# The second mixture's first 128 rows computed with w1 as the moving operand, and a split of the scatters ahead of them

## The chip, the cores and the metric

The kernel runs on one core of one Trainium2 chip. The metric is the device time of one execution in microseconds (us), the median of several executions. Before the change it is 572.95 us, the median of 3 runs (572.11 to 574.3).

## What is computed

Three stages follow each other: a decayed linear attention, a mixture of experts with one expert for each token, and a second such mixture in which tokens with a positive skip score are computed and the others pass through.

```python
def _attn_ref(q, k, v, alpha):            # B, H, S, D = 4, 8, 768, 48
    for t in range(S):
        state = alpha[:, :, t, :, None] * state + einsum('bhd,bhe->bhde', k[:, :, t], v[:, :, t])
        y[:, :, t] = einsum('bhd,bhde->bhe', q[:, :, t], state)

def _moe_ref(x, w_gate, w_output_gate, w1, w2):   # 3072 tokens, D 384, 8 experts, F 1024
    e_idx = argmax(x @ w_gate, axis=1)
    for e in range(E):
        mask = e_idx == e
        ye = np.maximum(x[mask] @ w1[e], 0.0) @ w2[e]
        out[mask] = gate_w[mask, None] * eom[mask, e, None] * ye

def _moe2_ref(x, w_skip, w_gate, w1, w2):
    out = x.copy(); xc = x[x @ w_skip > 0]        # only these are computed
    # the same routing; y[mask] = gate_w * (relu(xc[mask] @ w1[e]) @ w2[e]); out = xc + y
```

## The kernel before

The attention takes the first 150 us or so, in chunks of 128 positions. While it ends, tokens are routed, and each token's row (384 values, its weight and its index) is scattered by GpSimd's indirect DMA to its expert's region of a buffer in HBM: `scr1` for the first mixture, `scr2` for the second. Both mixtures then work through one list, `ITEMS`. An item is a number of rows of one expert: load them (`load_rows`, a DMA of SyncE's queue, L368), transpose and split them in a high and a low part (`xsplit`, or `xsplit_small` for items with one row block, L404 on TensorE, L405 and L406 on ScalarE and VectorE), multiply by w1 and take the relu (layer 1), multiply by w2 (layer 2), and then the steps that follow. Every product is three: high by high, low by high, high by low.

Counted from zero, the items that matter here are these. Item 8 is expert 7 of the first mixture, the last one there, with 432 rows in 4 row blocks of 108. Item 9 is expert 0 of the second mixture, its first 128 rows. Item 10 is the next 128 rows of the same expert. Item 11 is expert 1 of the second mixture with 256 rows. Item 9's rows are loaded while item 8 is being computed, and none of them comes from item 8; rows of item 10 are among those that item 8's results are scattered to.

So there is a chain from item 8 to item 10, and it runs through item 9. `post1_steps` makes the steps that follow an item of the first mixture, in groups, and `stream` runs them inside the next item: group 0 ahead of layer 1, and each further group behind a piece of it. For item 8 (`quick`) the groups are: copy the result (`evac`); logits, row block 0 (`rows(0)`, L517 and L521), routing and weights; row blocks 1 and 2 and the places (`place`: the rank by small matmuls, L190 to L196, then the indices `pi`, L560, and `ski`); row block 3 and the scatters (L224), four to `scr2` and four to the output. Item 10's load stands on SyncE's queue behind the fourth scatter to `scr2`, and TensorE's transposes for item 10 (L404) stand behind item 9's layer 2.

Layer 1 has two forms. In the usual one (`layer1`, L431) a block of w1 is the stationary operand and the rows move: 8 blocks of F, each 9 matmuls of as many columns as there are rows, here 128. In the form by rows (`layer1_rows`, L449) the 128 rows are stationary and w1 moves: 2 halves of F, each 9 matmuls of 512 columns. Its result lies with rows on the partitions, so it is copied (`hr`, L695) and each half is turned by 4 transposes (`layer1_turn`, L456, then `hh` L461 and `hl` L462). Before the change item 10 runs by rows, item 9 does not. Layer 2 (L487) is the same for both, 24 matmuls of 384 columns.

In a by-rows item the loop of `stream` runs group 1 behind the first half, group 2 behind the second, and group 3 inside layer 2, behind its first piece (f = 0); the usual form runs group g behind block g - 1 of F. The order on each engine is that in which the code is written; engines wait for each other by semaphores alone.

Of the kernel before, what the change touches and what calls it, by code (L numbers as in the profile page):

```python
# [51 lines left out]
def kernel(  # L52
# [170 lines left out]
    def scatter(dst, idx, j, src, pp, bound, key=None):  # L223
        ins = nc.gpsimd.indirect_dma_start(  # L224
            out=dst, out_offset=bass.IndirectOffsetOnAxis(ap=idx.bitcast(U32)[0:pp, j:j + 1], axis=0),
            in_=src, in_offset=None, bounds_check=bound, oob_is_err=False,
        )
        if key is not None:
            if groups[key]:
                tc.declare_no_dep(ins.ins, group=key, reason="the rows differ")  # L230
            tc.add_to_no_dep_group(key, ins.ins)
            groups[key].append(ins)
# [9 lines left out]
    def turn_logits(sm_ps, lt, gg, pp):  # L242
        nc.tensor.transpose(sm_ps[0:pp, 128:128 + gg * LW], lt[0:gg * LW, 0:pp], ident[0:gg * LW, 0:gg * LW])
# [121 lines left out]
    def load_into(xr, it, g0=0, g1=None):  # L365
        first, e, base, pp, gg = it
        r0, g1 = e * CAP + base, g1 or gg
        nc.sync.dma_start(  # L368
            out=xr[0:pp, 0:g1 - g0],
            in_=(scr1 if first else scr2)[r0:r0 + pp * gg, :].rearrange("(p g) d -> p g d", p=pp)[:, g0:g1],  # L370
        )

    def load_rows(it):
        xr = mp.tile([128, G1, PAY], F32, name="xr", bufs=2)
        load_into(xr, it)
        return xr
# [63 lines left out]
        )  # L440

    def in_rows(it):
        return it[4] == 1 and it[2] > 0

    def layer1_rows(ws, xhl, c, ph, k0, k1):
        terms = [(kb, w, x) for kb in range(KB) for w, x in ((ws[0], xhl[0]), (ws[1], xhl[0]), (ws[0], xhl[1]))]
# [45 lines left out]
    def post1_evac(py, it, quick):  # L492
        n = it[3] * it[4]
        yt = mp.tile([128, KB, N1], F32, name="yt")
        for d in range(KB):
            if quick and d == 1:
                nc.vector.tensor_copy(yt[:, d, 0:n], py[d])
            else:
                nc.scalar.activation(out=yt[:, d, 0:n], in_=py[d], func=AF.Copy)
        return yt  # L500

    def post1_logits(yt, it):
        pp, gg = it[3:]
        smp = psM.tile([128, 512], F32, name="smp")
        for d in range(KB):
            for g in range(gg):
                nc.tensor.matmul(  # L507
                    smp[g * LW:(g + 1) * LW, 0:pp], wg2s[:, d], yt[:, d, g * pp:(g + 1) * pp],
                    start=(d == 0), stop=(d == KB - 1),
                )  # L510
        return smp, take_logits(smp, gg, pp)
# [53 lines left out]
        count(pp, gg, oh, ohs2, "b")  # L565
        return ski, pi

    def post1_scatter(idx, x2, it, kb=None, ko=None):
        pp, gg = it[3:]
        ski, pi = idx  # L570
        for g in range(gg):
            scatter(scr2[:, :], pi, g, x2[0:pp, g, :], pp, E * CAP - 1, kb)
        for g in range(gg):
            scatter(out, ski, g, x2[0:pp, g, 0:DM], pp, NT - 1, ko)

    def post2(py, xr, it, key=None, groups_=None):
# [11 lines left out]
    def post1_steps(py, cols, it, kb=None, ko=None, quick=False):  # L588
        row = ecap if it[:2] != (True, E - 1) and kb is not None else ecl2
        c = {}  # L590

        def evac():
            if in_rows(it):
                pp = it[3]
                c["x2"] = rp.tile([128, G1, PAY], F32, name="x2")
                nc.scalar.activation(
                    out=c["x2"][0:pp, 0, 0:DM], in_=py[0], func=AF.Copy, scale=cols[0:pp, 0, 0:1]
                )
            else:
                c["yt"] = post1_evac(py, it, quick)  # L600

        def turn():
            pp = it[3]
            pt = psT.tile([128, 512], F32, name="pt")[:, 0:KB * pp]
            for d in range(KB):
                nc.tensor.transpose(
                    pt[:, d * pp:(d + 1) * pp], c["x2"][0:pp, 0, d * 128:(d + 1) * 128], ident[0:pp, 0:pp]
                )
            c["yt"] = mp.tile([128, KB, N1], F32, name="yt")
            nc.scalar.activation(  # L610
                out=c["yt"][:, :, 0:pp], in_=pt.rearrange("p (d n) -> p d n", d=KB), func=AF.Copy
            )

        def logits():
            c["smp"], c["lt"] = post1_logits(c["yt"], it)
            if not in_rows(it):
                c["x2"] = rp.tile([128, G1, PAY], F32, name="x2")

        def route_():
            turn_logits(c["smp"], c["lt"], it[4], it[3])  # L620
            c["rt"] = post1_route(c["smp"], cols, it)

        def rows(g):
            if g < it[4]:
                post1_rows(c["yt"], cols, c["x2"], it, g, quick or it[4] < G1 or g % 2 == 1)

        def place():
            c["ix"] = post1_place(c["smp"], cols, c["rt"], it, row)

        def weight():  # L630
            post1_weight(cols, c["x2"], c["rt"], it)

        def send():
            post1_scatter(c["ix"], c["x2"], it, kb, ko)

        def room():
            if it[1] == E - 2 and kb is not None:
                bump(ohs2, ecl2, c["smp"][0:1, 400:401], EARLY2)

        r0, r1, r2, r3 = (lambda g=g: rows(g) for g in range(4))  # L640
        if in_rows(it):
            return ((evac,), (turn,), (logits,), (route_,), (), (weight, place), (send,))
        if quick:
            return ((evac,), (logits, r0, route_, weight), (r1, r2, place), (r3, send))
        if it[4] < G1:
            return ((), (evac,), (logits,), (r0, route_), (), (r1,), (r2, weight, place), (send,))
        return ((), (evac,), (logits,), (route_, r0), (r1,), (r2, weight, place), (r3, send), (room,))

    def stream(ws, kb_, ko_, first_rows=None, hooks={}, hooks2={}):
# [18 lines left out]
        for m, it in enumerate(ITEMS):  # L668
            first, e, base, pp, gg = it
            nxt = ITEMS[m + 1] if m + 1 < len(ITEMS) else None  # L670
# [10 lines left out]
            late = nxt is not None and (nxt[2] or nxt[0] != first)  # L681
# [2 lines left out]
                fn()  # L684
            by_rows = in_rows(it)
            if by_rows:
                xr_n = load_rows(nxt)
                hr = mp.tile([128, FF], F32, name="hr")
                for c in range(2):
                    ph = psH.tile([128, 512], F32, name="ph")[0:pp]  # L690
                    layer1_rows(ws, xhl, c, ph, 0, 4)
                    if c:
                        layer1_turn(hr, hhl, 0, pp)
                    layer1_rows(ws, xhl, c, ph, 4, 3 * KB)
                    nc.scalar.activation(out=hr[0:pp, c * 512:(c + 1) * 512], in_=ph, func=AF.Relu)  # L695
                    for fn in steps[c + 1] if c + 1 < len(steps) else ():
                        fn()
            for f in range(0 if by_rows else FB):
# [7 lines left out]
                if f == 5 and nxt and not late:  # L706
                    xr_n = load_rows(nxt)
# [8 lines left out]
            for f in range(FB):  # L716
# [8 lines left out]
                if f == 0 and late:  # L725
                    xr_n = load_rows(nxt)
# [625 lines left out]
```

## Time and profile before

| what | value |
|---|---|
| median of the runs (3) | 572.95 us |
| the profiled execution: its time, its span | 574.67 us, 572.9 us |
| TensorE (PE) busy | 545.2 us, 95% |
| VectorE (DVE), ScalarE (ACT), GpSimd (POOL) busy | 66%, 54%, 34% |
| item 9 on PE | from 412.98 us to 428.15 us |
| item 10 on PE | from 428.15 us to 439.47 us |
| mean granted clock of TensorE | 0.974 |

The span is the time from the first to the last instruction in the profiled execution, and the 1.77 us beside it are start and end. Times inside the trace count from the start of the span. A row of the timeline says when an instruction (or a run of equal ones) began, how long it took until its result was there, and in brackets how long its engine had been idle and who ended that. Consecutive matmuls overlap, so the distance between their starts is what one costs in a row of them, and the duration is what a reader of the result waits for.

### The profile page before, as it was taken

Reading aid. Unit: us, or ns where it says so; the run is one execution under the profiler, and the core shown is the slowest. Engines: PE = TensorE matmul, PEld = TensorE weight load, DVE = VectorE, ACT = ScalarE, POOL = GpSimd, SP = SyncE. Lnnn points to the kernel's source line nnn. Section 1 sums busy time; section 2 is a strip of 40 time slices with the busy share of each in tenths; the row PEclk is TensorE's granted clock in tenths of the full one; section 3 lists DMA queues with packets and bytes.
Section 4 is the critical chain, followed back from the end, with each engine's and each line's share of the span. In section 5 each row is a group of like instructions: output and inputs, shape, how many; then the busy total and the mean of one; then the engine's idle time right before and its main releaser. Section 6 shows DMA issues by size and latency. Waiting matters only on the chain.

```text
span 572.9 us, 11819 instructions
## 1 busy us (share of the span) xinstructions
PE 545.2 (95%) x4546; PEld 497.0 (87%) x4546; DVE 375.4 (66%) x870; ACT 309.9 (54%) x723; POOL 194.2 (34%) x202
## 2 busy tenths in 40 slices
PE   6899997979999999999999999999999999999993
PEld 5788776867797899999999999999998999999993
DVE  7899899997464454737465554737466677776740
ACT  3575756865445454656464544645355666555630
POOL 5432645565122631533517072503251011110111
PEclk8599999998999999999999999999999999999997
DMA  8975656232793464472727364442636665676600
GB/s 321 401 286 201 247 192 243 84 116 102 255 303 114 165 208 135 159 266 73 266 85 256 112 238 135 146 167 58 216 93 218 229 217 186 212 241 226 200 21 22
DMA packets 34358, 106.21 MB, mean 185 GB/s; under 512 B 7735, under 2 KB 11506, under 8 KB 34293
## 3 DMA queue, kind: packets, MB, share of 16 engines
q1 hardware_dynamic: 25845, 92.82, 47.5%
q0 software_dynamic: 8448, 12.55, 6.3%
q8 instruction: 37, 0.61, 0.4%
q14 instruction: 28, 0.23, 0.1%
HBM read 88.96 MB, written 27.13 MB: 203 GB/s over the span
## 4 chain that ended last, share of the span: by engine, by line
PE 77%; DVE 14%; DMA 3%; issue 2%; ACT 2%; POOL 1%; SPq 0%; POOLq 0%; DVEq 0%; ACTq 0%
PE ph L431 28%; PE py L478 19%; PE py L487 11%; PE py L431 3%; DVE P L922 3%; PE pt L387 2%; DVE r L947 2%; PE ps L970 2%; DVE A L977 2%; PE pt L517 2%; PE py L1024 2%; DVE k L949 2%; PE py L1030 1%; DVE qp L958 1%; PE smp L507 1%
## 5 line engine op out<-in xcount | busy, mean ns | idle before, releaser
L224 POOL DMA_INDIRECT scr<-x,pi x56 | 68.6, 1225 | 155.0 <-DVE osb L207 84.2
L431 PE MATMUL ph<-xh,w1h 128*128 128x432 f32 (+3 forms) x330 | 109.7, 333 | 0.0
L431 PE MATMUL ph<-xl,w1h 128*128 128x432 f32 (+3 forms) x330 | 106.3, 322 | 0.3 <-DVE xl L392 0.3
L431 PE MATMUL ph<-xh,w1l 128*128 128x432 f32 (+3 forms) x330 | 106.1, 321 | 0.0
L437 DVE SCALAR_TENSOR_TENSOR hl<-ph,hh 128x432 fp32r<-128x432 f32 (+3 forms) x110 | 56.3, 511 | 66.4 <-ACT hh L436 65.9
L436 ACT ACTIVATE hh<-ph 128x432 fp32r<-128x432 f32 (+3 forms) x110 | 50.2, 457 | 80.1 <-PE ph L431 79.0
L336 DVE TENSOR_TENSOR w2l<-st,w2h 128x512 fp32r<-128x512 f32 x96 | 64.2, 688 | 43.9 <-ACT w2h L334 43.8
L334 ACT ACTIVATE w2h<-st 128x512 fp32r<-128x512 f32 x96 | 57.9, 626 | 45.8 <-DMA st<-in_w2a_dram 26.2
L478 PE MATMUL py<-hh,w2h 128*128 128x432 f32 (+1 forms) x192 | 69.1, 360 | 0.0
L336 DVE TENSOR_TENSOR w1l<-st,w1h 128x512 fp32r<-128x512 f32 x96 | 65.0, 707 | 6.1 <-ACT w1h L334 4.4
L478 PE MATMUL py<-hh,w2l 128*128 128x432 f32 (+1 forms) x192 | 67.4, 351 | 0.0
L478 PE MATMUL py<-hl,w2h 128*128 128x432 f32 (+1 forms) x192 | 67.4, 351 | 0.0
L431 PEld LDWEIGHTS ph<-xh,w1h 128*128 128x128 f32 x330 | 62.3, 189 | 2.4 <-issue 1.2
L431 PEld LDWEIGHTS ph<-xl,w1h 128*128 128x128 f32 x330 | 62.2, 188 | 2.3 <-DVE xl L392 0.7
L431 PEld LDWEIGHTS ph<-xh,w1l 128*128 128x128 f32 x330 | 62.3, 189 | 1.0
L334 ACT ACTIVATE w1h<-st 128x512 fp32r<-128x512 f32 x96 | 56.3, 623 | 2.6 <-DMA st<-in_w1a_dram 2.6
L224 POOL DMA_INDIRECT out_dram<-ot,ti x16 | 15.6, 976 | 119.6 <-DVE ot L582 109.2
L487 PE MATMUL py<-w2h,hh 128*128 128x384 f32 (+1 forms) x136 | 48.3, 355 | 0.0
L487 PE MATMUL py<-w2l,hh 128*128 128x384 f32 (+1 forms) x136 | 45.8, 337 | 0.0
L940 POOL TENSOR_TENSOR t<-P,r 112x512 f32<-112x512 f32 x22 | 28.1, 1275 | 49.6 <-DVE P L922 43.5
L487 PE MATMUL py<-w2h,hl 128*128 128x384 f32 (+1 forms) x136 | 43.8, 337 | 0.0
L970 PE MATMUL ps<-qp,k 48*128 48x128 f32 x384 | 34.0, 310 | 7.5 <-DVE A L977 4.8
(226 smaller groups left out, 1108.3 us busy)
## 6 DMA issues: line engine op xcount, KB each, us to landing
st<-in_w1a_dram SPq DMA_DIRECT2D x24, 512.0 KB, 4.5
st<-in_w2a_dram SPq DMA_DIRECT2D x24, 512.0 KB, 5.1
st<-in_w1b_dram SPq DMA_DIRECT2D x24, 512.0 KB, 4.2
st<-in_w2b_dram SPq DMA_DIRECT2D x24, 512.0 KB, 3.5
x<-in_ad_dram SPq DMA_DIRECT2D x8, 774.0 KB, 6.2
ain<-in_ad_dram SPq DMA_DIRECT2D x7, 774.0 KB, 7.7
kin<-in_kd_dram SPq DMA_DIRECT2D x7, 768.0 KB, 7.6
qin<-in_qd_dram SPq DMA_DIRECT2D x7, 768.0 KB, 9.0
```

The costliest lines, as they stand in the source:

```text
L224: ins = nc.gpsimd.indirect_dma_start(out=dst, out_offset=bass.IndirectOffsetOnAxis(ap=idx.bitcast(U32)[0:pp, j:j + 1], axis=0), in_=src, i ...
L334: nc.scalar.activation(out=hi, in_=src, func=AF.Copy)
L336: nc.vector.tensor_tensor(out=lo, in0=src, in1=hi.bitcast(F32), op=ALU.subtract)
L387: nc.tensor.transpose(pt[:, g * pp:(g + 1) * pp], rows_of(xr, g)[0:pp, kb * 128:(kb + 1) * 128], ident[0:pp, 0:pp])
L431: nc.tensor.matmul(ph[:, 0:n], w[:, kb, f * 128:(f + 1) * 128], x[:, kb, 0:n], start=(k == 0), stop=(k == 3 * KB - 1),)
L436: nc.scalar.activation(out=hh[:, f, 0:n], in_=ph[:, 0:n], func=AF.Relu)
L437: nc.vector.scalar_tensor_tensor(out=hl[:, f, 0:n], in0=ph[:, 0:n], scalar=0.0, in1=hh[:, f, 0:n].bitcast(F32), op0=ALU.max, op1=ALU.subtract,
L478: nc.tensor.matmul(py[d], w[:, f, dsl], hx[:, f, 0:pp * gg], start=(f == 0 and k == 0), stop=(f == FB - 1 and k == 2),)
L487: nc.tensor.matmul(py[g], hx[:, f, gsl], w[:, f, :], start=(f == 0 and k == 0), stop=(f == FB - 1 and k == 2),)
L922: scans[i] = nc.vector.tensor_tensor_scan(out=P.rearrange("p a b -> p (a b)"), data0=a[0:PR, c].rearrange("p a b -> p (a b)"), data1=floor ...
L940: ti = (nc.gpsimd if i > 1 else nc.vector).tensor_tensor(out=t, in0=P, in1=r, op=ALU.mult)
L970: nc.tensor.matmul(pss[j][:, hp], k2[rr, hp], qp[rr, hp])
```

## The change

`in_rows` now holds for item 9 too, so its layer 1 takes the form by rows, and the groups of item 8's steps move to that form's places. `load_rows(nxt)` at the head of a by-rows item is left out where the next item's rows must be loaded late, so item 10's load stays at f = 0 of layer 2, now behind group 3. `post1_scatter` can send a part of the row blocks; group 2 of item 8's steps ends with the scatters of row blocks 0 to 2 to `scr2` (`send_0`), and group 3 sends row block 3 there and then all four to the output (`send_1`).

```diff
     def in_rows(it):
-        return it[4] == 1 and it[2] > 0
+        return it[4] == 1 and (it[2] > 0 or not it[0])
...
-    def post1_scatter(idx, x2, it, kb=None, ko=None):
+    def post1_scatter(idx, x2, it, kb=None, ko=None, to_scr=None, to_out=None):
...
-        for g in range(gg):
+        for g in range(gg) if to_scr is None else to_scr:
             scatter(scr2[:, :], pi, g, x2[0:pp, g, :], pp, E * CAP - 1, kb)
-        for g in range(gg):
+        for g in range(gg) if to_out is None else to_out:
             scatter(out, ski, g, x2[0:pp, g, 0:DM], pp, NT - 1, ko)
...
+        def send_0():
+            post1_scatter(c["ix"], c["x2"], it, kb, ko, range(it[4] - 1), ())
+
+        def send_1():
+            post1_scatter(c["ix"], c["x2"], it, kb, ko, (it[4] - 1,))
...
         if quick:
-            return ((evac,), (logits, r0, route_, weight), (r1, r2, place), (r3, send))
+            return ((evac,), (logits, r0, route_, weight), (r1, r2, place, send_0), (r3, send_1))
...
             if by_rows:
-                xr_n = load_rows(nxt)
+                if not late:
+                    xr_n = load_rows(nxt)
```

The first place is TensorE in item 9, between group 1 and group 2 of item 8's steps. L517 are the transposes of row blocks 1 and 2, L190 begins the rank. Before:

```order
L431 MATMUL ph<-xh,w1h_5008 128x128
L431 MATMUL ph<-xh,w1l_5009 128x128
L431 MATMUL ph<-xl,w1h_5008 128x128
L517 MATMUL pt<-ident,yt 108x128 x6
L190 LDWEIGHTS onesb
L190 MATMUL smp<-ecl_87,onesb 108x32
```

With the change:

```order
L449 MATMUL ph<-w1h_5008,xh 128x512
L456 MATMUL pt<-ident,hr 128x128 x4
L449 MATMUL ph<-w1l_5009,xh 128x512
L449 MATMUL ph<-w1h_5008,xl 128x512
L449 MATMUL ph<-w1h_5008,xh 128x512
L449 MATMUL ph<-w1l_5009,xh 128x512
L449 MATMUL ph<-w1h_5008,xl 128x512
L517 MATMUL pt<-ident,yt 108x128 x6
L190 LDWEIGHTS onesb
L190 MATMUL smp<-ecl_87,onesb 108x32
```

Ahead of the rank there stood 18 matmuls of 128 columns, and now there stand 18 of 512 columns and 4 transposes.

The second place is GpSimd, at item 8's scatters (`scr_78` is `scr2`, the numbers are the program's). Before:

```order
L224 DMA out_dram<-x_5063,ski 3072x384 x4
L224 DMA scr_78<-x_5392,pi_5457 28080x388 x4
L224 DMA out_dram<-x_5392,ski 3072x384 x4
L224 DMA out_dram<-ot,ti_5641 3072x384
L224 DMA out_dram<-ot,ti_5751 3072x384
```

With the change:

```order
L224 DMA out_dram<-x_5063,ski 3072x384 x4
L224 DMA scr_78<-x_5392,pi_5463 28080x388 x4
L224 DMA out_dram<-x_5392,ski 3072x384 x4
L224 DMA out_dram<-ot,ti_5582 3072x384
L224 DMA out_dram<-ot,ti_5692 3072x384
```

On this engine nothing moved: the scatters follow each other as they did.

## Rows read from the trace of the kernel before

**Rows 1.** The page's part 4: shares of the chain that ended last.

```profile
PE 77%; DVE 14%; DMA 3%; issue 2%; ACT 2%; POOL 1%; SPq 0%; POOLq 0%; DVEq 0%; ACTq 0%
```

**Rows 2.** Windows: stretch, us, busy us of PE, PEld, DVE, ACT, POOL, granted clock, DMA.

```profile
412.98:428.15 15.17, 15.17 (x141) 14.40 (x140) 8.48 (x34) 8.58 (x21) 7.17 (x7) 1.00 0.33 87
439.47:565.00 125.53, 123.69 (x885) 122.20 (x884) 85.64 (x191) 66.73 (x148) 14.26 (x15) 1.00 0.57 187
```

**Rows 3.** Timeline of PE, item 9: start us, us, instruction.

```profile
412.98 0.22 PE L431 MATMUL ph<-xh,w1h 128*128 128x128 f32 x1
...
415.24 0.30 PE L431 MATMUL ph<-xh,w1h 128*128 128x128 f32 x1
...
416.28 0.83 PE L517 MATMUL pt<-ident,yt 128*108 128x128 f32 x6
417.04 0.27 PE L190 MATMUL smp<-ecl,onesb 1*108 1x32 bf16 x2
...
417.51 0.31 PE L431 MATMUL py<-xh,w1h 128*128 128x128 f32 x1
...
427.76 0.34 PE L487 MATMUL py<-w2l,hh 128*128 128x384 f32 x1
427.94 0.34 PE L487 MATMUL py<-w2h,hl 128*128 128x384 f32 x1
428.15 0.41 PE L404 MATMUL pt<-ident,xr 128*128 128x128 f32 x2
```

**Rows 4.** Timeline of DVE, POOL and SyncE's queue, from item 8's indices on.

```profile
418.14 0.16 DVE L560 TENSOR_TENSOR pi<-pos,nb 108x4 int32<-108x4 f32 x1
...
419.15 0.99 POOL L224 DMA_INDIRECT scr<-x,pi  x1 [12.95 <-ACT hh L436]
...
423.04 0.99 POOL L224 DMA_INDIRECT scr<-x,pi  x1 [0.30 <-issue]
...
425.67 0.33 SPq L368 DMA_DIRECT2D xr<-scr  x1
...
430.16 0.33 SPq L368 DMA_DIRECT2D xr<-scr  x1
```

**Rows 5.** Timeline of PE, item 10, which runs by rows.

```profile
429.22 0.40 PE L449 MATMUL ph<-w1l,xh 128*128 128x512 f32 x1
...
431.77 0.40 PE L449 MATMUL ph<-w1h,xh 128*128 128x512 f32 x1
432.00 0.60 PE L456 MATMUL pt<-ident,hr 128*128 128x128 f32 x4
432.36 0.47 PE L449 MATMUL ph<-w1l,xh 128*128 128x512 f32 x1
432.67 0.39 PE L449 MATMUL ph<-w1h,xl 128*128 128x512 f32 x1
...
435.11 0.34 PE L487 MATMUL py<-w2l,hh 128*128 128x384 f32 x1
435.60 0.41 PE L387 MATMUL pt<-ident,xr 128*128 128x128 f32 x2
```

**Rows 6.** Windows: the two stretches before the end with the lower clock.

```profile
10.80:27.86 17.06, 15.00 (x122) 12.94 (x124) 14.98 (x21) 7.97 (x20) 8.99 (x23) 0.50 1.02 403
126.85:133.68 6.83, 6.50 (x70) 5.34 (x71) 5.00 (x10) 4.11 (x13) 4.50 (x3) 0.50 0.65 233
```

**Rows 7.** Timeline of PE: matmuls behind rests, in brackets the rest.

```profile
10.93 1.44 PE L970 MATMUL ps<-qp,k 48*128 48x128 f32 x10 [2.38 <-DVE k L949]
...
93.69 0.17 PE L190 MATMUL smp<-ecap,onesb 1*128 1x32 bf16 x1 [1.60 <-DVE lo L250]
...
126.23 1.01 PE L970 MATMUL ps<-qp,k 48*128 48x128 f32 x4 [1.35 <-DVE A L977]
```

**Rows 8.** Groups by form, from 10.8 to 27.86 us and from 27.87 to 40 us.

```profile
L970 PE MATMUL ps<-qp,k 48*128 48x128 f32 x48 | 6.9, 439 | 4.3 <-DVE k L949 2.4 <-DVE A L977 1.9
...
L970 PE MATMUL ps<-qp,k 48*128 48x128 f32 x46 | 3.4, 285 | 0.0
```

## The prediction

> **What bounds the kernel now.** I read the chain of what ended last first: TensorE has 77% of it [rows 1]. The windows then show where: from item 11 on, PE is busy 123.69 of 125.53 us, at the full clock [rows 2], and what is missing is the end behind the last matmul. So what makes item 11 start later or earlier moves the end by as much, and nothing behind it gives time back. Items 9 and 10 have to be read closely, since PE is busy all through item 9 as well (15.17 of 15.17 us) and a list of waits would show nothing there.
>
> The timeline shows two things that end almost together before item 10. PE's last layer 2 matmul of item 9 starts at 427.94, one step of 0.18 us (427.76 to 427.94) behind the one ahead of it, so PE is free at 428.1; the transposes of item 10's rows start at 428.15 [rows 3]. The rows themselves come by a chain that begins on PE, too: the transposes of item 8's row blocks 1 and 2 at 416.28, the rank at 417.04 [rows 3], the indices on DVE at 418.14, the first scatter on POOL at 419.15 and the fourth at 423.04 (three steps of 1.30), item 10's load on SyncE's queue at 425.67 when that scatter has landed [rows 4], and PE at 428.15, 2.48 us after that issue. From 416.28 to 428.15 the chain takes 11.87 us, of which PE's own part is 1.23 (416.28 to 417.51). PE's work of item 9 and the chain end within 0.1 us of each other: whichever the change makes longer sets item 10's start.
>
> **The order of item 9's work.** Both depend on when the steps of item 8 get their turn. Before r1 and r2 (the transposes at 416.28) there stand two runs of nine narrow matmuls. One run takes 1.04 us (415.24 to 416.28) [rows 3], both 2.08. With the change 18 matmuls of 512 columns stand there. Item 10 shows their price, since it has the same shape: eleven steps from 429.22 to 431.77 are 2.55 us, 0.232 each [rows 5], so 18 take 4.17. The four transposes between them take 0.36 (432.00 to 432.36), and the first matmul behind them 0.31 to the next instead of 0.23 [rows 5], 0.44 together. That is 4.61 for 2.08: **the steps come 2.53 us later**, and with them rank, scatters, landing and load. One wait is new: there are two buffers for transposes, the first turned half occupies one, and row block 2's transposes need it, so they wait until VectorE has read that half, behind the routing. The trace has no such wait. The turn stands 1.6 us ahead of r1 (0.36 + 0.31 + four times 0.232), which should nearly do; the bounds are nothing and one row block's own transposes, half of 416.28 to 417.04, 0.4. I take 0.1, so 2.6 with bounds of 2.5 and 2.9.
>
> **What PE saves.** The eight narrow runs of layer 1 go, 8 times 1.04 = 8.3, and 4.17 + 2 times 0.44 = 5.05 come: 3.3 us less by that, and 2.7 if the second turn waits for its copies and row block 3's transposes for ScalarE, as the turns in item 10 do by tenths. PE would be through with item 9 at 425.0 to 425.5 instead of 428.1. None of it counts if the rows land at 428.15 + 2.6 = 430.75: PE then rests some 5.4 us. What hid the chain is the cover that the change takes away.
>
> **The scatters.** POOL's rows in the order of before and of the change are the same, since four scatters to `scr2` already stood ahead of those to the output, and each waits for its own row block. The first waits for the indices (418.14) and starts at 419.15, before row block 3 can matter, and they are 1.30 us apart [rows 4]. Written ahead of row block 3 or behind, they start when they did in relation to the rank. Cost and gain: nothing, unless ScalarE's copies were late; at 1.30 us for a scatter the fourth has 3.9 us to spare.
>
> **What stands behind the waits.** On SyncE's queue the load waits until 428.3, and three loads of expert 1's w2 stand behind it; they are wanted in item 10's layer 2, 7 us after its start, and lose nothing. Item 11's rows come last on that queue, at 430.16, behind item 9's output [rows 4]. Before, they were late: PE's step at 435.11 should be followed at 435.28, and the transposes came at 435.60 [rows 5], 0.32 us of wait. With the change the w2 loads are out earlier in relation to item 10, so I take 0.3 off; the bounds are 0.3 and nothing. The splits of w1 that move ahead on ScalarE and VectorE, the copies by halves and the turn's readers lie beside layer 2 and PE's rest, and cost nothing while that rest is there.
>
> **The clock.** A rest of 5.4 us is longer than any in this trace between the first and the last matmul. Behind a rest of 2.38 us PE's first matmul comes at 10.93, and the granted clock is 0.50 from 10.80 on, for 17.06 us; behind one of 1.35 us at 126.23 it is 0.50 from 126.85 on, for 6.83 us; a rest of 1.60 us at 93.69 has no such consequence [rows 6, 7]. [...] If the fall comes 2.3 us into the rest, as at 10.80, and lasts 6.83 us as the second did, 3.1 us lie in the rest and 3.7 on item 10's matmuls: 1.8 us lost. The bounds are nothing and 3.4 (all 6.83 on work). I take 1.8: item 10 is denser work than what followed the first fall, where PE rested for 2.06 of the 17.06 us [rows 6], so the second fall is the nearer row.
>
> [...]
>
> **The sum.** 2.6 for the later rows, less 0.3 for item 11's rows, and 1.8 for the clock: **4.1 us slower**. The profiled execution has a span of 572.9, which becomes 577.0, and with the 1.8 us around it 578.8 for 574.67. Its time stands 1.7 above the median of the runs, so I carry the difference over and not the sum: 572.95 + 4.1 = **577.1 us**.
>
> **The rivals.**
> *The clock stays.* If the rest falls so that the lower level ends with it, or never comes, 2.3 us remain: 575.3. For it: the rest of 1.60 us without a fall. Against it: this rest is over twice the longest one that the trace has.
> *PE decides, and the kernel is faster.* If the rows are there when PE is through with item 9, its saving counts: 572.95 - 2.7 = 570.3. For it speaks that before the change PE shows no wait for item 10's load worth naming. The place is the transposes of item 10 (L404), the price 2.7 us, and it decides from the point where the chain from r1 to the landing takes no more than about 6.5 us (418.9 to 425.4); it takes 11.87, and its parts on POOL and in the queues are not touched, so it would have to lose nearly half. [...]
> *A long fall.* If the lower clock holds for 17.06 us on work, as long as the first did, 8.5 us are lost: 572.95 + 2.3 + 8.5 = 583.8. Against it: PE was busy 15.00 of those 17.06 us only [rows 6], and item 10 has short waits alone.
> *Nothing happens.* The part with the scatters does nothing; for the whole change that would need a chain that doesn't begin behind layer 1's matmuls, and PE's order shows that it does: 573.
>
> **How the numbers follow.** Forecast 0.72, the clock stays 0.14, PE decides 0.04, a long fall 0.06, nothing 0.04. A measurement of this kernel can tell about 0.5%, 2.9 us, from no change. Slower by more than that are the long fall and the forecast where the clock takes at least 0.6 us, which I hold for 0.64 of its 0.72: 0.70 in all. Within it are the kept clock, nothing, the rest of the forecast, and most of the case in which PE decides (2.7 us): 0.28. Faster remains 0.02. The range takes in the forecast's own bounds, 572.95 + 2.2 to 572.95 + 2.6 + 3.4 = 575.2 to 579.0, the kept clock, and about 1 us on both sides, since the runs shown lie between 572.11 and 574.3: 574.4 to 580.0. It leaves out about one and a half in ten.
>
> **What would show it.** In the profile of the changed kernel r1 and r2 stand 2.6 us later behind item 9's first matmul, 5.9 instead of 3.3; the first scatter again 2.9 us behind them; PE has one rest of about 5.4 us that item 10's load ends; a stretch of granted clock 0.50 begins in or just behind that rest; item 11's rows are no longer waited for; from item 11 on all is as before. The forecast is wrong if PE's rest at L404 is short (then the chain shrank, and I mis-sized it), or if item 10's matmuls keep their 0.232 us throughout (then only 2.3 us are left).

## The result and the profile after

The changed kernel takes **579.11 us** (median, 577.47 to 580.43), the kernel before 573.32 beside it: **1.0101** times as long, with a 95% interval of 1.0061 to 1.0141. The profiled execution has 580.43 us with a span of 578.7, for 574.67 and 572.9. Four executions that stand far above the others of their kernel are left out of the ratios further down: three of before and one of e2, which took 2898.81 us. The 5.8 us between the spans are all in items 9 and 10. Item 9's first matmul starts 0.70 later (413.68 for 412.98), from there to item 11's first matmul it is 32.36 us for 26.49, and from there to the end 132.66 for 133.43: 0.70 + 5.87 - 0.77 = 5.8.

The page's part 4 shows a chain with less TensorE in it, against [rows 1]:

```profile
PE 73%; DVE 15%; DMA 4%; issue 3%; POOL 2%; ACT 2%; POOLq 0%; SPq 0%; DVEq 0%
```

The windows (columns as in [rows 2]) are item 9 up to item 10's transposes, item 10 up to item 11's first matmul, the stretch of granted clock 0.50 between them, and both items in one. In [rows 2] item 9 had 15.17 us, and PE was busy in all of them; now PE works 12.64 of 19.13. The work got shorter and the stretch longer.

```profile
413.68:432.81 19.13, 12.64 (x96) 10.33 (x94) 8.06 (x28) 8.64 (x17) 7.98 (x7) 0.94 0.25 71
432.81:446.04 13.23, 13.09 (x60) 10.55 (x61) 5.67 (x14) 6.75 (x16) 1.99 (x2) 0.82 0.48 168
430.65:437.47 6.82, 4.66 (x12) 3.52 (x13) 1.27 (x5) 0.65 (x3) 3.59 (x4) 0.50 0.90 298
413.68:446.04 32.36, 25.74 (x155) 20.89 (x154) 13.73 (x42) 15.39 (x33) 9.97 (x9) 0.89 0.34 111
```

The timeline of PE answers to [rows 3] and [rows 5]: item 8's r1 and r2 at 419.69, the rank at 420.64, the end of item 9's layer 2 at 425.46, then the rest of 6.49 us that item 10's rows end. Item 10's matmuls stand 0.43 us apart from 434.27 to 437.26 and 0.23 behind that. In brackets is the rest ahead of a row and what ended it.

```profile
413.68 0.40 PE L449 MATMUL ph<-w1h,xh 128*128 128x512 f32 x1
...
419.69 1.02 PE L517 MATMUL pt<-ident,yt 128*108 128x128 f32 x6
420.64 0.27 PE L190 MATMUL smp<-ecl,onesb 1*108 1x32 bf16 x2
...
425.46 0.86 PE L487 MATMUL py<-w2h,hl 128*128 128x384 f32 x4
432.81 0.66 PE L404 MATMUL pt<-ident,xr 128*128 128x128 f32 x2 [6.49 <-DMA xr<-scr]
...
433.68 0.79 PE L449 MATMUL ph<-w1h,xh 128*128 128x512 f32 x1
434.27 0.63 PE L449 MATMUL ph<-w1l,xh 128*128 128x512 f32 x1
...
437.26 0.50 PE L449 MATMUL ph<-w1h,xl 128*128 128x512 f32 x1
437.59 0.40 PE L449 MATMUL ph<-w1h,xh 128*128 128x512 f32 x1
...
444.01 0.44 PE L387 MATMUL pt<-ident,xr 128*128 128x128 f32 x2
```

The timelines of DVE, POOL and SyncE's queue answer to [rows 4]. The third and fourth scatter take 1.50 us, where all four took 0.99, and they lie beside the six subtractions that make w1's low halves (L336, 424.11 to 427.80). The second lies beside them too, from 424.11 on, and kept its 1.00.

```profile
421.75 0.16 DVE L560 TENSOR_TENSOR pi<-pos,nb 108x4 int32<-108x4 f32 x1
...
424.11 3.69 DVE L336 TENSOR_TENSOR w1l<-st,w1h 128x512 fp32r<-128x512 f32 x6
...
422.75 0.99 POOL L224 DMA_INDIRECT scr<-x,pi  x1 [15.44 <-ACT x L521]
424.05 1.00 POOL L224 DMA_INDIRECT scr<-x,pi  x1 [0.30 <-ACT w1h L334]
425.35 1.50 POOL L224 DMA_INDIRECT scr<-x,pi  x1 [0.30 <-ACT w1h L334]
427.16 1.50 POOL L224 DMA_INDIRECT scr<-x,pi  x1 [0.30 <-issue]
...
430.32 0.33 SPq L368 DMA_DIRECT2D xr<-scr  x1
```

Counted from item 9's first matmul, in us:

| | before | after | later by |
|---|---|---|---|
| r1 and r2 (L517) | 3.30 | 6.01 | 2.71 |
| rank (L190) | 4.06 | 6.96 | 2.90 |
| first scatter | 6.17 | 9.07 | 2.90 |
| fourth scatter | 10.06 | 13.48 | 3.42 |
| load (L368) | 12.69 | 16.64 | 3.95 |
| item 10's transposes (L404) | 15.17 | 19.13 | 3.96 |
| item 11's first matmul | 26.49 | 32.36 | 5.87 |

Each step of this table suggests a cause: 2.71 for the wider matmuls ahead of r1, 0.19 for r2's buffer, 0.52 and 0.53 more for the longer scatters (the fourth starts later and takes longer), and 1.91 in item 10, where the clock is low. What stayed to be tested is whether these are separate causes or one that shows in several places, and whether the clock follows the rest.

### The profile page after: what moved, and what is told of

Read it like the earlier page. It is cut to its first block, busy times and chain, and to the rows that moved or that the text cites. A ratio compares the mean times of both kernels' runs of the same rounds, so it can differ in the third digit from the quotient of the medians.

```text
span 578.7 us, 11719 instructions
## 1 busy us (share of the span) xinstructions
PE 542.6 (94%) x4500; PEld 492.9 (85%) x4500; DVE 374.8 (65%) x864; ACT 309.4 (53%) x719; POOL 196.3 (34%) x202
## 2 busy tenths in 40 slices
DMA packets 34358, 106.21 MB, mean 184 GB/s; under 512 B 7735, under 2 KB 11506, under 8 KB 34293
## 4 chain that ended last, share of the span: by engine, by line
PE 73%; DVE 15%; DMA 4%; issue 3%; POOL 2%; ACT 2%; POOLq 0%; SPq 0%; DVEq 0%
PE ph L431 26%; PE py L478 17%; PE py L487 12%; DVE P L929 3%; PE py L431 3%; DVE r L954 3%; PE ph L449 3%; DVE A L984 2%; PE pt L387 2%; PE pt L517 2%; DVE k L956 2%; DVE qp L965 1%; DMA scr<-x,pi 1%; PE ps L977 1%; DMA xr<-scr 1%
## 5 line engine op out<-in xcount | busy, mean ns | idle before, releaser
L431 PE MATMUL ph<-xh,w1h 128*128 128x432 f32 (+2 forms) x312 | 104.7, 336 | 0.0
L431 PE MATMUL ph<-xl,w1h 128*128 128x432 f32 (+2 forms) x312 | 101.1, 324 | 0.0
L431 PE MATMUL ph<-xh,w1l 128*128 128x432 f32 (+2 forms) x312 | 101.1, 324 | 0.0
L437 DVE SCALAR_TENSOR_TENSOR hl<-ph,hh 128x432 fp32r<-128x432 f32 (+2 forms) x104 | 54.5, 524 | 63.1 <-ACT hh L436 62.6
L336 DVE TENSOR_TENSOR w2l<-st,w2h 128x512 fp32r<-128x512 f32 x96 | 64.1, 686 | 42.2 <-ACT w2h L334 42.2
L436 ACT ACTIVATE hh<-ph 128x432 fp32r<-128x432 f32 (+2 forms) x104 | 48.6, 467 | 78.4 <-PE ph L431 77.4
L334 ACT ACTIVATE w2h<-st 128x512 fp32r<-128x512 f32 x96 | 57.8, 625 | 44.2 <-DMA st<-in_w2a_dram 26.5
L336 DVE TENSOR_TENSOR w1l<-st,w1h 128x512 fp32r<-128x512 f32 x96 | 65.0, 707 | 7.3 <-ACT w1h L334 5.7
L431 PEld LDWEIGHTS ph<-xh,w1h 128*128 128x128 f32 x312 | 58.8, 188 | 2.4 <-issue 1.2
L431 PEld LDWEIGHTS ph<-xl,w1h 128*128 128x128 f32 x312 | 58.7, 188 | 1.8 <-DVE xl L392 0.2
L431 PEld LDWEIGHTS ph<-xh,w1l 128*128 128x128 f32 x312 | 58.9, 189 | 1.0
L334 ACT ACTIVATE w1h<-st 128x512 fp32r<-128x512 f32 x96 | 56.3, 623 | 4.0 <-DMA st<-in_w1a_dram 4.0
```

Source lines behind the costliest of these rows:

```text
L334: nc.scalar.activation(out=hi, in_=src, func=AF.Copy)
L336: nc.vector.tensor_tensor(out=lo, in0=src, in1=hi.bitcast(F32), op=ALU.subtract)
L431: nc.tensor.matmul(ph[:, 0:n], w[:, kb, f * 128:(f + 1) * 128], x[:, kb, 0:n], start=(k == 0), stop=(k == 3 * KB - 1),)
L436: nc.scalar.activation(out=hh[:, f, 0:n], in_=ph[:, 0:n], func=AF.Relu)
L437: nc.vector.scalar_tensor_tensor(out=hl[:, f, 0:n], in0=ph[:, 0:n], scalar=0.0, in1=hh[:, f, 0:n].bitcast(F32), op0=ALU.max, op1=ALU.subtract,
```

## The experiments

The runs were made in three groups, each on a chip of its own, and the kernel before was timed beside every group. It took 581.27 us in the first group (a0, e1, e2, e3), 582.34 in the second (b0, e4, e5, e6) and 573.92 in the third (b1, a1, e5 again, b2). Ratios are to before of the same group.

### The change again, on another chip

The changed kernel, unedited.

> The changed kernel once more, to stand beside the others on one chip. Theory: 5 to 6 us slower than before; r1 and r2 (the transposes of row blocks 1 and 2) 6.0 us behind item 9's first matmul, a rest of PE of 6 to 6.5 us ahead of item 10, the fourth scatter 4.4 us behind the first, and a stretch of granted clock 0.50 that takes about 1.9 us from item 10. Rival (the 5.8 us are chance of a chip): under 3 us.

582.15 us, ratio 1.0025 (1.0000 to 1.0050). The stretch of items 9 and 10 is 32.72 us, with the same steps to within 0.02 us up to the load and scatters of 0.99, 1.00, 1.51 and 1.50. By the time the rival holds (0.9 us), by the trace the theory: the loss sits where it did in the first pair, while nearly all of the difference to before is gone. On this chip the change is 3.0 us slower than in the first pair and the kernel before 8.0; the controls below take that up.

### Item 8's steps early, item 9 by rows (e1)

In item 9 the steps of group 1 (logits, row block 0, routing and weights) come behind the first four wide matmuls instead of behind the ninth, and those of group 2 (r1, r2, the places and three scatters) behind the ninth instead of the eighteenth.

```diff
+                    elif late:
+                        for fn in steps[1]:
+                            fn()
                     layer1_rows(ws, xhl, c, ph, 4, 3 * KB)
                     nc.scalar.activation(out=hr[0:pp, c * 512:(c + 1) * 512], in_=ph, func=AF.Relu)
+                    if late:
+                        for fn in steps[2] if c == 0 else ():
```

> Item 9 by rows as in the change, but item 8's groups of steps earlier: logits and routing behind 4 of the first 9 wide matmuls, row blocks 1 and 2 and the rank behind the 9th. Theory (it is the place of the steps): r1 at 3.3 to 3.5 us behind item 9's first matmul as before the change, item 10's load and transposes at 15.2 to 16.0, PE's rest 2.5 to 3.3 us; the time within 2 us of before, by as much as the clock falls. Rival (the wide form of item 9 itself, or what it does to the loads, costs the time): 4 us or more slower, as in the change.

579.22 us, ratio 0.9962 (0.9934 to 0.9991), 2.9 us under the change on the same chip. r1 and r2 stand 3.50 us behind item 9's first matmul, the four scatters take 0.99 each, and item 10's transposes come at 15.39, which is 0.2 us behind before's 15.17. Two of the three causes are gone with one move. TensorE still rests for 2.95 us, since its own work of item 9 is shorter, and the clock falls all the same:

```profile
413.15:442.25 29.10, 26.01 (x154) 21.34 (x154) 13.80 (x42) 15.38 (x33) 9.94 (x9) 0.88 0.39 122
427.50:434.40 6.90, 5.86 (x15) 4.43 (x16) 1.27 (x5) 1.24 (x4) 3.48 (x4) 0.51 0.99 340
```

The windows are both items and the low stretch. Of the 2.6 us that the two items take over before's 26.49, 2.4 are item 10's (13.72 for 11.32). In the low stretch 5.86 of 6.90 us are work; e5 below has item 10 at the same place without a fall, in 11.38 us.

### Item 8's steps late, item 9 in its usual form (e2)

The kernel before, with the groups of item 8 put behind item 9's second, fifth and sixth narrow run instead of the first, second and third.

```diff
-                for fn in steps[f + 1] if f + 1 < len(steps) else ():
+                g = {1: 1, 4: 2, 5: 3}.get(f, 99) if not first and e == 0 else f + 1
+                for fn in steps[g] if g < len(steps) else ():
```

> The kernel before with item 9 in the usual form, but item 8's groups later: group 1 behind the second block of F, group 2 behind the fifth, group 3 behind the sixth. Theory (place of the steps): r1 at 6.3 us instead of 3.3, item 10's transposes 3 us later than before (18.2 us behind item 9's first matmul) or 4 with scatters slowed by the splits, PE's rest 3 to 4 us, 3 us slower and up to 5 with the clock. Rival (the wide form): nothing moves, within 0.5 us of before.

581.89 us, ratio 1.0014 (0.9982 to 1.0045): beside a before of 581.27 the time shows nothing. In the trace, lateness alone costs what the sum gave it: r1 and r2 at 6.32 for 3.30, transposes at 18.18 for 15.17, the two items 29.49 us for 26.49.

```profile
412.56:442.05 29.49, 26.26 (x200) 23.47 (x199) 14.67 (x48) 15.30 (x37) 9.45 (x9) 1.00 0.38 122
```
```profile
418.88 0.83 PE L517 MATMUL pt<-ident,yt 128*108 128x128 f32 x6
...
430.74 0.41 PE L404 MATMUL pt<-ident,xr 128*128 128x128 f32 x2 [2.88 <-DMA xr<-scr]
```

The first line is the window of both items, the others are rows of PE. PE rests for 2.88 us, as long as in e1, and the granted clock of the window is 1.00: no fall. So the length of the rest by itself doesn't decide.

### The rest filled with matmuls (e3)

The change, with 22 matmuls of 512 columns ahead of item 10's transposes. Nothing reads their result: they are added work.

```diff
+                if f == FB - 1 and (first, e, base) == (False, 0, 0):
+                    pw = psM.tile([128, 512], F32, name="smp")
+                    for _ in range(22):
+                        nc.tensor.matmul(pw, ws[0][:, 0, 0:128], ws[0][:, 0, 0:512])
```

> The change, with 22 matmuls of 512 columns put on PE between item 9's layer 2 and item 10's transposes, whose result nobody reads: 5.1 us of the 6.5 us of rest. Theory (the clock takes 1.9 us of it): granted clock 1.00 through item 10, its wide matmuls 0.23 us apart, item 10 at the same distance from item 9 as in the change, and 1.9 us faster than the change, 3.5 to 4 slower than before. Rival (the clock takes nothing, the lateness all): the same time as the change. A second rival (the matmuls outlast the wait): slower than the change.

580.83 us, ratio 0.9999 (0.9971 to 1.0026), 1.3 us under the change on the same chip, with intervals that overlap. The rest shrank to 1.52 us, and the clock fell in spite of it, for half as long, which neither the theory nor the rivals had:

```profile
436.50:439.90 3.40, 3.40 (x9) 2.66 (x8) 0.69 (x3) 0.11 (x1) 1.00 (x1) 0.50 1.02 363
```
```profile
435.21 0.41 PE L404 MATMUL pt<-ident,xr 128*128 128x128 f32 x2 [1.52 <-DMA xr<-scr]
```

Item 10 took 12.88 us for the 13.48 of the change on that chip. Filling the rest gave 0.6 us and not the 1.9 that the clock costs, since the low stretch, though shorter, now fell wholly on work.

### The subtractions behind the scatters (e4)

The change, with the six subtractions of w1 (L336) on VectorE, and the weight loads that wait for them, put behind item 10's copies. ScalarE's halves of the splits (L334) stay.

```diff
+                if held:
+                    later.append((wn, i, u, pieces[i]))
+                    split_half(wn, i, u, pieces[i], "h")
+                    halves += 1
+                    return
                 split_half(wn, i, u, pieces[i])
@@
                         xsplit_small(xr_n, nxt, xhl_n)
+                        for w_, i_, u_, st_ in later:
+                            split_half(w_, i_, u_, st_, "l")
```

> The change, with the six VectorE subtractions that split expert 1's w1 moved from beside the scatters to behind item 10's rows (ScalarE's copies stay; the loads of w2 that need the buffers come later, so the total isn't read). Theory (VectorE's work beside them makes scatters longer): all four scatters take 0.99 us and stand 1.30 apart, the fourth 12.9 to 13.0 us behind item 9's first matmul instead of 13.48, item 10's transposes at 18.1 to 18.2 instead of 19.13. Rival (scatters are longer there because of DMA traffic or ScalarE): 1.50 us for the last two as in the change, transposes at 19.1.

585.54 us in one execution, so the time says little. Item 10 got slow in this kernel (17.87 us): its wide matmuls stand 0.43 us apart from 434.56 to 436.69, as at the clock of 0.50 in the change, and item 11's rows stand on SyncE's queue behind weight loads that now come late, so that ScalarE's first copy of them (L391, 445.04) waits 2.40 us for PE's transposes. What it is for is POOL's timeline:

```profile
424.08 0.99 POOL L224 DMA_INDIRECT scr<-x,pi  x1 [15.89 <-ACT x L521]
425.37 0.99 POOL L224 DMA_INDIRECT scr<-x,pi  x1 [0.30 <-issue]
426.67 0.99 POOL L224 DMA_INDIRECT scr<-x,pi  x1 [0.30 <-issue]
427.96 0.99 POOL L224 DMA_INDIRECT scr<-x,pi  x1 [0.30 <-issue]
```

The scatters are back at 0.99 us and 1.30 apart, at the same late place (the first 9.07 us behind item 9's first matmul, as in the change). The load comes 15.59 us behind it, 1.05 earlier than in the change, and PE's rest is 1.05 us shorter (5.44). So VectorE's subtractions beside the scatters cost the chain 1.05 us, and ScalarE's halves, which still run beside the second and third, cost nothing. DMA traffic is out as well: beside the third scatter it is 60 GB/s over 1.81 us in the change and 84 over 1.29 here, the same amount, and in neither trace is a load issued among the four.

### The subtractions beside the scatters, in the kernel before (e6)

The other way round: before, with w1's splits beginning at item 9's third narrow run and item 10's load issued there, too.

```diff
-            l1 = ((4, 5, 6, 7) if first else ()) if (e, base) == (0, 0) else ((3, 5, 6, 7) if pp * gg == N1 else (1, 3, 5, 7))
+            l1 = ((4, 5, 6, 7) if first else (2, 3, 4, 5, 6, 7)) if (e, base) == (0, 0) else ((3, 5, 6, 7) if pp * gg == N1 else (1, 3, 5, 7))
@@
+                if f == 2 and (first, e, base) == (False, 0, 0):
+                    xr_n = load_rows(nxt)
                 if f in l1:
-                    split_next(12)
+                    split_next(12 if first or e or base else 6)
```

> The kernel before (item 9 in the usual form, steps at their places), with the six splits of expert 1's w1 put into item 9's layer 1, beside the scatters, and item 10's load ahead of the next loads in the queue. Theory (VectorE's work beside them makes scatters longer): two or three of the four scatters take 1.3 to 1.5 us, the fourth stands 10.5 to 11.2 us behind item 9's first matmul instead of 10.06, item 10's transposes at 15.9 to 16.7 instead of 15.18. Rival: scatters of 0.99, transposes at 15.2.

578.41 us, ratio 0.9927 (0.9891 to 0.9963). The second and third scatter are now long:

```profile
419.89 0.99 POOL L224 DMA_INDIRECT scr<-x,pi  x1 [12.50 <-ACT hh L436]
421.19 1.33 POOL L224 DMA_INDIRECT scr<-x,pi  x1 [0.30 <-ACT hh L436]
422.83 1.35 POOL L224 DMA_INDIRECT scr<-x,pi  x1 [0.31 <-ACT w1h L334]
424.49 0.99 POOL L224 DMA_INDIRECT scr<-x,pi  x1 [0.30 <-issue]
```

The fourth starts at 10.77 for 10.06, the load at 13.43 for 12.69, and PE rests for 0.68 us that it didn't rest before. The same subtractions that cost the change 1.05 us cost before 0.7 when they are put there, so the price hangs on their place beside the scatters and not on the wide form. The fourth scatter stayed at 0.99 although a subtraction runs beside it: not every one is lengthened. The ratio under 1 is not a gain of this edit in items 9 and 10 as the first pair would have it (27.46 us for 26.49); before must lose time on this chip that this version does not lose, and the control below shows one such loss.

### Steps early and a shorter filling (e5)

e1 with 8 of e3's matmuls, whose result nothing reads, in the rest that e1 leaves.

> The early steps with item 9 by rows, and 8 matmuls of 512 columns (1.9 us of the 2.95 us of rest) whose result nobody reads. Theory (the clock is what this version still loses): item 10 at 15.4 us behind item 9, 11.3 us long at the full clock, so items 9 and 10 in 26.7, as before the change (26.5). Rival (a short rest is enough for the lower clock): item 10 takes 12.8 us or more.

576.25 us, ratio 0.9889 (0.9844 to 0.9933). PE's rest is 1.15 us, the clock doesn't fall (item 10's wide matmuls stand 0.23 us apart), and the two items take 26.82 us: 0.33 more than before has in the first pair. Item 10 starts at 15.44 us, as in e1 (15.39), and takes 11.38 for 13.72, so the fall alone cost e1 2.3 us. With the steps in their place and the clock kept, the change's loss in items 9 and 10 is undone. Nothing is won, although PE's needed work is shorter, since the rows of item 10 set its start as they did.

### Before again: the difference that vanished on one chip

The kernel before, unedited, in the second group.

> The kernel before as a kernel of its own, for its trace on the chip of the others and as a measure of what the comparison itself scatters. Theory: ratio 1.000 within 0.3%; items 9 and 10 take 15.2 and 11.3 us as in the first trace, and what differs between chips and executions lies ahead of item 9, in the attention stage. Rival (on another chip item 10's load is later in the kernel before, too, so that the change has less to lose): item 10 starts 18 us or more behind item 9, or the clock falls there.

581.20 us, ratio to its own other runs 0.9976 (0.9947 to 1.0005), no difference, as it has to be. Its trace shows one way in which before can be slow itself. In items 9 and 10 it took 30.37 us, not 26.49, and the reason is on ScalarE. The rows are three of ScalarE and two of PE:

```profile
426.84 0.28 ACT L436 ACTIVATE hh<-ph 128x128 fp32r<-128x128 f32 x1 [1.10 <-PE ph L431]
430.37 0.28 ACT L436 ACTIVATE hh<-ph 128x128 fp32r<-128x128 f32 x1 [3.26 <-remote]
430.55 3.22 ACT L334 ACTIVATE w1h<-st 128x512 fp32r<-128x512 f32 x6
...
427.15 0.27 PE L431 MATMUL ph<-xl,w1h 128*128 128x128 f32 x1
...
434.58 0.50 PE L449 MATMUL ph<-w1h,xh 128*128 128x512 f32 x1 [2.45 <-ACT xh L405]
```

PE's last narrow matmul starts at 427.15 and the activation that reads it at 430.37, behind a rest of 3.26 us that no tile of the program explains. The last update of PE's semaphore that the trace holds ahead of it is at 430.35, 3.20 us behind the start of that matmul; what held it up isn't shown. The six splits of w1 stand behind it, item 10's copies behind those, and PE waits 2.45 us for the copies at 434.58; the clock then is low: the granted one is 0.94 over both items, and the wide matmuls stand 0.43 us apart from 435.75 on.

Call such a late start a standstill. Ahead of item 9 all kernels are the same, so their traces can be laid beside the first one of before, instruction by instruction. In each of the eight profiles of the first two groups three to six instructions of ScalarE there begin 0.7 to 3.8 us later, behind the instruction that releases them, than they do in that trace; in the other five profiles none does. Three of them lie close together between 190 and 202 us, and the one at L239 comes behind a rest of ScalarE of 1.63 to 2.31 us in each of the eight, where the rest is 0.20 in the six others. In items 9 and 10 only the control has one: e2 and e6, which also have item 9 in the usual form, took 29.49 and 27.46 us there without any.

Rests that a profile puts down to "issue" or "remote" are no measure of this. There are 11 to 17 of over 0.5 us on ScalarE and 9 to 12 on VectorE in each of the eight, and one and none in the six, but most are ordinary waits whose end is not in the trace: the control's holds 1750 updates of the semaphores of PE, ScalarE and VectorE, that of before 1879. An example is ScalarE's copy (L391) of what PE turned, in the control and, below it, in the first trace of before:

```profile
249.14 0.53 PE L387 MATMUL pt<-ident,xr 108*128 108x108 f32 x4
249.77 0.53 ACT L391 ACTIVATE xh<-pt 128x432 fp32r<-128x432 f32 x1 [2.16 <-issue]
```
```profile
246.37 0.53 ACT L391 ACTIVATE xh<-pt 128x432 fp32r<-128x432 f32 x1 [2.09 <-PE pt L387]
```

The rest is about as long in both, and in the control the copy begins 0.10 us behind the end of PE's row.

From item 0's first matmul to item 9's first it is 260.5 and 261.1 us in the first pair, 262.5 to 266.3 in the eight, and 260.1 to 262.9 in the four of the third group, falls of the clock included.

Two things were open: whether this is a matter of the chip or of one execution, and whether the change's loss comes back where there are no standstills. The third group put before twice, the change and e5 on one chip.

> The kernel before, unedited, once more with a profile. Open: why the change costs 1.0101 in the first pair and only 1.0025 on another chip, although the stretch from item 9's first matmul to item 11's first is as long there (32.72 us) as in the first pair (32.36). Theory: before itself is longer there, because ScalarE stood still for 3.26 us ahead of one hh of item 9 in the control (430.37), which sent the w1 splits and item 10's copies late: items 9 and 10 took 30.37 us in place of 26.49. If the theory holds, this execution again shows a standstill of ScalarE or VectorE of 2 to 4 us in items 9 and 10 that no tile explains, and 29.5 to 31 us for the two items. Rival: the control's standstill was an accident of one execution; then the two items take 26.5 us here, and the missing difference is elsewhere (in the attention ahead of item 9, or behind item 11).

> The changed kernel, unedited, timed on the same chip as the other runs of this group. Theory (standstill in before, which the change's ScalarE, with less to do in item 9, does not have on the path): items 9 and 10 take 32.4 to 32.8 us, 1.5 to 3 us over before on the same chip, and the ratio is 1.002 to 1.006. Rival (accident): the two items differ by 5.9 us as in the first pair, and the ratio is 1.008 to 1.012. If ScalarE and VectorE show no standstills on this chip at all, both say 1.010.

> e5 again (item 9 by rows with item 8's steps at the 4 and 9 wide matmuls, and 8 matmuls that nothing reads in TensorE's rest): does it beat both kernels on the same chip as both? Both theories: items 9 and 10 in 26.8 us, against 32.5 of the change; ratio to before 0.986 to 0.995 if before has the standstill, 0.999 to 1.002 if it has not.

> The kernel before, a second look on this chip, for the same question as the first: theory, again a standstill of 2 to 4 us on ScalarE or VectorE in items 9 and 10, at the same place or another, and 29.5 to 31 us for the two items; rival, 26.5 us.

On this chip none of the four profiles has a standstill. Before takes 573.92 us, the change 579.10, ratio **1.0089** (1.0055 to 1.0123), and e5 574.35, ratio 1.0006 (0.9981 to 1.0030). The windows of both items, in the order before (two executions, of 576.56 and 571.26 us), the change and e5:

```profile
415.03:441.74 26.71, 26.22 (x200) 23.54 (x199) 14.65 (x48) 15.05 (x37) 9.86 (x9) 1.00 0.42 134
```
```profile
409.56:436.36 26.80, 26.18 (x200) 23.53 (x200) 14.72 (x48) 15.13 (x37) 9.88 (x9) 1.00 0.44 135
```
```profile
412.85:445.02 32.17, 25.54 (x155) 20.75 (x153) 13.74 (x42) 15.39 (x33) 9.96 (x9) 0.89 0.36 112
```
```profile
413.02:439.76 26.74, 25.33 (x163) 20.91 (x162) 13.81 (x42) 15.37 (x33) 9.96 (x9) 1.00 0.41 133
```

The change has 32.17 us again, 5.4 over before, and the times differ by 5.2. The result of the first pair is therefore the kernel's. The 1.0025 was measured on a chip whose profiles have standstills, and they may add more to before than to the change; that is not shown. Neither theory on the control was put to the test by the third group, since it has no standstills; the one in items 9 and 10 was seen in one profile only. For its recurrence speaks that the profiles of the change and of the control differ by 2.35 us in the two items (32.72 and 30.37) and by 1.2 in all, near the measured 0.9, though they are of two chips. Against it speak e2 and e6, which have none there. e5 beats the change on the chip where both were timed (574.35 for 579.10); it beats before in the second group and equals it in the third.

The part of the change with the scatters has no run of its own. A kernel with that part alone has the order of before on every engine, so no difference is to be expected; that is argued and not measured.

## Why the prediction was right, and where it was not

The forecast was 577.1 us, slower, and the kernel took 579.11, slower, within the range of 574.4 to 580.0. The mechanism held: item 8's steps come later, the rows of item 10 with them, PE rests, and the clock falls into item 10. Against the terms of the sum:

| term | forecast | measured |
|---|---|---|
| 18 wide matmuls ahead of r1 | 2.53 | 2.71 |
| r2's wait for a buffer | 0.1 (0 to 0.4) | 0.19 |
| scatters, and splits of w1 beside them | 0 | 1.05 |
| item 11's rows no longer waited for | -0.3 | 0 |
| the clock | 1.8 (0 to 3.4) | 1.9 |
| both items | 4.1 | 5.87 |

**The step that failed** is that "the splits of w1 that move ahead on ScalarE and VectorE" would "cost nothing while that rest is there". The forecast sought their price on VectorE, ScalarE and PE, where they do lie beside a rest. Their price is on GpSimd: the third and fourth scatter take 1.50 us beside the subtractions. e4 takes 1.05 us back by moving the subtractions and the loads that follow them, and e6 makes it appear in the kernel before. The trace of before had it in plain sight, two scatters further on. There the subtractions lay beside the scatters to the output, on which nothing waits:

```profile
424.89 3.70 DVE L336 TENSOR_TENSOR w1l<-st,w1h 128x512 fp32r<-128x512 f32 x6 [0.23 <-ACT w1h L334]
...
424.33 0.99 POOL L224 DMA_INDIRECT out_dram<-x,ski  x1 [0.30 <-issue]
425.63 1.42 POOL L224 DMA_INDIRECT out_dram<-x,ski  x1 [0.30 <-issue]
427.36 1.50 POOL L224 DMA_INDIRECT out_dram<-x,ski  x1 [0.30 <-issue]
```

I read the scatters' price from the four at 0.99 [rows 4] and didn't ask which rows lay beside them, and which would after the change. In the change the same subtractions begin 10.43 us behind item 9's first matmul (11.91 before), while the scatters to `scr2` begin 2.9 us later, and the two meet.

**The clock** was forecast by the nearer of two falls [rows 6], and its length came out the same, 6.82 us for 6.83. It fell 4.3 us into the rest and not 2.3, and 4.66 us of it were work, where the forecast had 3.7. By the forecast's own step, half of the work (1.8 of 3.7), that is 2.3 us, so that 1.8 came this near to the 1.9 is in part luck. That half is what the rows at the two clocks show: one matmul of the attention takes 0.144 us at 0.50 (48 in 6.9) and 0.074 at 1.00 (46 in 3.4) [rows 8], and item 10's wide ones in the change stand 0.43 us apart at 0.50 and 0.23 behind it. The two earlier falls stood behind waits for VectorE [rows 7], this one, of 6.49 us, behind a wait for a DMA; e2's wait for the same DMA, of 2.88 us, had none behind it. Item 10's first eight steps, which took 1.96 us before (428.88 to 430.84), took 3.58, from 433.68 to 437.26: 1.62 of the 1.9. That this is the clock and not lateness is shown by e2, which is nearly as late (18.18 us for 19.13) and has no fall (item 10 in 11.32 us), and by e1, which is hardly late and has one (13.72; 11.38 in e5, without it).

**The rest of PE** was forecast at 5.4 us and is 6.49; 1.05 of the difference is the scatters. PE's own saving came out a little under the forecast's 2.7 to 3.3 (which end item 9 at 424.8 to 425.4, not at 425.0 to 425.5): 12.64 us of work for 15.17, 2.5 less, and none of it counts.

**Item 11's rows.** The 0.32 us of [rows 5] are gone, as I said, and another wait of 0.30 took their place: the third transposes of item 11 start 0.47 us behind the matmul ahead of them (443.54 to 444.01) instead of 0.17. The term should have been nothing.

**The rivals.** "The clock stays" fell with the window 430.65 to 437.47, and "a long fall" with its 6.82 us. "PE decides" and "nothing happens" fell with the rest of 6.49. All five terms came out too small, and the sum is 1.8 us short; 1.35 of that are the scatters and item 11's rows. That the time still fell within the range is owed to the width that it gave the clock and the runs; the forecast had no term for longer scatters.

## What to carry to other kernels

Where a change moves work on one engine, look at what will newly run beside it on the others, and search the old trace for the same pair side by side: here its price stood two rows below the rows I used. When a chain on another engine ends together with the work above it, as here, making the work shorter buys nothing (2.5 us of PE's here); the steps that start the chain have to keep their distance from its beginning, as e1 and e5 do it (transposes at 15.39 and 15.44 us for 15.17). A kernel's loss should be measured on more than one chip: this one's is 1.0101, 1.0025 and 1.0089 in three comparisons, with 32.2 to 32.7 us in items 9 and 10 in each.

## What the runs showed of the hardware

**Scatters beside subtractions.** In the two profiles of the first pair, behind 180 us, 75 scatters by GpSimd have no weight subtraction (L336) beside them, and the longest of these took 1.01 us. Of 76 with subtractions in more than half of their first microsecond 35 took over 1.2. In e2 two scatters to `scr2` stayed at 0.99 and 1.00 beside them, as did the change's second, so it is frequent and not certain; what decides in the single case is open.

**The clock and rests.** Rests of 2.88 us (e2) and 2.95 us (e1) ended one without and one with a fall, and a rest of 1.52 us behind added matmuls was followed by one (e3), one of 1.15 us was not (e5). What tells them apart isn't settled by these runs.

**Standstills.** On two of the chips three to six instructions of ScalarE in an execution begin 0.7 to 3.8 us late behind what releases them, ahead of item 9, and the kernel before took 581 to 582 us in place of 573 to 574. Some lie at the same instructions in all eight profiles (L239 and L436, near 195 us). The traces of these chips also lack semaphore updates, so that ordinary waits stand there as "issue". The DMA packets are the same to within one in the profiles of before, the change, the control, e4, e5 and e6 (34358, and 34359 in e5). Whether the standstills make up the 8 us, and their cause, stays open.
